# Linear attention and a two-layer MLP on one core: bf16 weights by GpSimd's DMA queue, filler matmuls and a new scheduler model

## The chip, the core and the metric

The kernel runs on one core of a Trainium2 chip. Every time in this document is device time in microseconds (us), from the start of the program to its end on that core; durations of single instructions are sometimes in nanoseconds (ns). Times of a kernel are medians of several executions. A profile is one further execution, recorded by the hardware profiler.

## The reference

Two parts are computed one after the other. The first is a linear attention with a state that decays (4 batches, 8 heads, 768 positions, 48 elements for each head); the second is an MLP over all 3072 tokens, with 384 inputs, 2048 hidden elements and 384 outputs. The inputs and outputs are float32.

```python
# attention, for every batch and head
for t in range(S):                                   # S = 768
    cur   = u * k[t] (outer) v[t]
    y[t]  = r[t] @ (state + cur)
    state = w[:, None] * state + k[t] (outer) v[t]
x = y.transpose(0, 2, 1, 3).reshape(3072, 384)

# MLP
h = x @ w_in                                         # 384 -> 2048
g = where(h >= 1, h, where(h <= -1, 0, (h + 1)**2 / 4))
out = g @ w_out                                      # 2048 -> 384
```

## The kernel before

The sequence is cut into chunks of 128 positions. A chunk of one batch is a *unit*; there are 24. In a unit, K is multiplied by inverse powers of w and R by powers of w; the products are transposed (`KR` to `RK`), the 128 x 128 scores are computed, masked (`AT`) and multiplied by V, the contribution of the state is added (`Tbd`), and a term on the diagonal with u (`VD`). The result `x` is transposed to `xT`. Two units make a block of 256 tokens; there are 12 blocks, and each block takes 8 groups of layer 1 (6 matmuls each) and 8 groups of layer 2 (4 matmuls each). The MLP uses the middle branch, (h + 1)^2 / 4, for everything; bounds on the norms are computed beside it, and the whole MLP is done again with clipping if they don't exclude an |h| above 1.

The first eight units ("soft") transpose on TensorE; the other sixteen transpose by DMA.

The order of all instructions is fixed when the kernel is built. Each operation is entered with the engines that may run it, its estimated time on each, its dependences, its buffers and a time at which it is due. A list scheduler (`Plan.run`) simulates the engines and picks engine, buffer and position. On the chip, each engine then runs its instructions in that order and waits on semaphores.

```python
# the scheduler's picture of a DMA
if o.dma is not None:
    issue = est + occ
    if len(dmas) >= 2:
        issue = max(issue, dmas[-2])
    begin = max(dma_end, issue + 0.3)
    dma_end = begin + o.dma
    ...
    o.end = dma_end + 1.7
```

```python
# constants: four loads of single 4-byte words on ScalarE's queue
def tiny(dst, src):
    for s in range(2):
        nc.scalar.dma_start(out=dst[halves[s], :], in_=src.rearrange("(p s) d -> s d p", s=2)[s])
...
tiny(wraw, w); tiny(uraw, u)

# loads of a unit (L326), SyncE's queue
nc.sync.dma_start(out=t, in_=src[b, :, t0 : t0 + C, :].rearrange("h s d -> s h d"))

# weights: float32 into a buffer (L349, L363), then a cast by DVE, ACT or POOL (L242)
ORDER = ["U0", "U1", "I0", "I1", "U2", "I2", "I3", "U3", "U4", "O0", "U5", "O1", "U6", "O2", "U7", "O3"]
t = get(bf, [128, nKb, FQ], F32)
nc.sync.dma_start(out=t, in_=w_in_src[:, :, q * FQ : (q + 1) * FQ])
...
copy(e, w_in_sb[:, kk, q * FQ : (q + 1) * FQ], bf.t[:, kk, :])
```

```python
# attention (cut): the engines that may run each step
o_kw = P.op(f"kw{i}", both, ...)                     # L390, DVE or POOL
o_rw = P.op(f"rw{i}", both, ...)                     # L394, DVE or POOL
o_v  = P.op(f"v{i}", {DVE, ACT, POOL}, ...)          # L242 V<-Vf
nc.tensor.transpose(trb.t[:, p, :], pair(krb.t, p), ident)            # L409, soft units
mm(at_p[s].t[:, p, :], rkb.t[halves[s], NP + p, :], rkb.t[halves[s], p, :], ...)   # L429, scores
nc.vector.tensor_mul(atb.t[s], at_p[s].t, umask4)                     # L435, mask
mm(pair(y, p), rkb.t[:, p, :], Tbd[b][:, p, :], ...)                  # L485, state
mm(y[:, h, :], atb.t[h % 2][:, h // 2, :], vb.t[:, h, :], ...)        # L488
mm(stb.t[:, p, :], pair(krb.t[:, H:, :], p), pair(vb.t, p), ...)      # L536, new state
o_bd = P.op(f"bd{i}", {ACT, POOL, DVE}, ...)         # L242 Tbd<-T

# MLP (cut)
mm(hb.t[:, f, :], w_in_sb[...], xT[m][:, kk, :], ...)                 # L574, layer 1
nc.scalar.activation(gb[m].t[...], hb.t, AF.Square, bias=0.5, scale=0.5)   # L586
mm(ob.t, gb[m].t[...], w_out_sb[:, f, :], ...)                        # L597, layer 2
copy(e, osb.t, ob.t)                                                  # L242 os<-o
nc.sync.dma_start(out=out[t0 : t0 + C, :], in_=osb.t)                 # L611
```

Of the kernel before, what the change touches and what calls it, by code (L numbers as in the profile page):

```python
# [8 lines left out]
F32 = mybir.dt.float32  # L9
# [5 lines left out]
SEM = 0.06  # L15


class Buf:
    def __init__(self, pool):
        self.pool, self.users, self.slot, self.t = pool, [], None, None  # L20


class Op:
    def __init__(self, name, engs, fn, deps, uses, allocs, due, dma, after, nb):
        self.name, self.engs, self.fn, self.due, self.dma = name, engs, fn, due, dma
        self.after, self.nb = [a for a in after if a], nb
        self.deps, self.uses, self.allocs = [d for d in deps if d], list(uses), list(allocs)
        self.eng = self.start = self.end = None
        for b in self.uses + self.allocs:
            b.users.append(self)  # L30


class Plan:
# [6 lines left out]
    def op(self, name, engs, fn, deps=(), uses=(), allocs=(), due=0.0, dma=None, after=(), nb=0.0):  # L40
        o = Op(name, engs, fn, deps, uses, allocs, due, dma, after, nb)
        self.ops.append(o)
        return o
# [22 lines left out]
    def run(self):  # L66
        free = dict.fromkeys(("PE", "ACT", "DVE", "POOL", "SP", "ACTQ"), 0.0)
        dmas, dma_end = [], 0.0
        todo, done, last_mlp = list(self.ops), [], "L2"
        while todo:  # L70
            cand = []
            for o in todo:
                if any(d.start is None for d in o.deps) or any(a.start is None for a in o.after):
                    continue
                pl = self.place(o) if o.allocs else (0.0, [])
                if pl is None:
                    continue
                ready = max([d.end + SEM for d in o.deps] + [a.start + 0.001 for a in o.after] + [pl[0], o.nb])
                for e in o.engs:
                    cand.append((max(free[e], ready), ready, o, e, pl[1]))  # L80
            if not cand:
                raise RuntimeError("no operation can be placed: " + ", ".join(o.name for o in todo[:12]))
# [23 lines left out]
            if o.dma is not None:  # L106
                issue = est + occ
                if len(dmas) >= 2:
                    issue = max(issue, dmas[-2])
                begin = max(dma_end, issue + 0.3)  # L110
                dma_end = begin + o.dma
                dmas.append(dma_end)
                free[e] = issue
                o.end = dma_end + 1.7
            else:
                free[e] = est + occ
                o.end = est + lat
# [8 lines left out]
def pe(t):  # L126
    return {"PE": (t, t + 0.17)}
# [22 lines left out]
def kernel(  # L150
# [11 lines left out]
    nc = tc.nc  # L162
# [16 lines left out]
    NS = 8  # L179
# [12 lines left out]
    P = Plan(slots)  # L192

# [11 lines left out]
    def row_bcast(src):  # L205
        return bass.AP(tensor=src.tensor, offset=src.offset, ap=[[0, 128], [1, H * D]])
# [3 lines left out]
    wraw = const.tile([128, NP], F32, name="wraw")  # L210
    uraw = const.tile([128, NP], F32, name="uraw")
# [36 lines left out]
    def tiny(dst, src):  # L248
        with nc.allow_non_contiguous_dma(reason="384 words"):
            for s in range(2):  # L250
                nc.scalar.dma_start(out=dst[halves[s], :], in_=src.rearrange("(p s) d -> s d p", s=2)[s])

    c_wbc = P.op("c_wbc", {"ACT": (0.6, 2.5)}, lambda e: nc.scalar.dma_start(out=w_bc, in_=row_bcast(w)), due=-100)
    c_cols = P.op("c_col", {"POOL": (0.2, 0.2)}, lambda e: nc.gpsimd.iota(i_int, pattern=[[0, 1]], base=0, channel_multiplier=1), due=-100)

    def f_kr(i):
        def fn(e):
            nc.vector.memset(KR[i], 0.0)
        return fn

    kr0 = [P.op(f"c_kr{i}", {"DVE": (0.35, 0.4)}, f_kr(i), due=-90 + i if i < 2 else 0) for i in range(slots["KR"])]

# [3 lines left out]
    c_icol = P.op("c_icol", {"DVE": (0.3, 0.35)}, f_col, deps=[c_cols], due=-99)  # L266
# [10 lines left out]
    def f_wu(e):  # L277
        nc.vector.memset(wraw, 1.0)
        nc.vector.memset(uraw, 1.0)
        nc.vector.memset(ones, 1.0)  # L280
    c_wu0 = P.op("c_wu0", {"DVE": (0.3, 0.3)}, f_wu, due=-95)

    def f_wu1(e):
        tiny(wraw, w)
        tiny(uraw, u)
    c_wu = P.op("c_wu", {"ACT": (1.8, 4.0)}, f_wu1, deps=[c_wu0], due=-99)
    c_ubc = P.op("c_ubc", {"ACT": (0.6, 4.5)}, lambda e: nc.scalar.dma_start(out=u_bc, in_=row_bcast(u)), due=-94)
# [5 lines left out]
    def f_wc(e):  # L293
        nc.scalar.activation(wc, wraw, AF.Ln)
        nc.scalar.activation(wc, wc, AF.Exp, scale=float(C))
    c_wc = P.op("c_wc", {"ACT": (0.45, 0.5)}, f_wc, deps=[c_wu], due=11)

    def f_uw(e):
        nc.gpsimd.memset(uw, 0.0)
        for s in range(2):  # L300
            nc.gpsimd.tensor_mul(uw[halves[s], :, s], wraw[halves[s]], uraw[halves[s]])
    c_uw = P.op("c_uw", {"POOL": (0.5, 0.5)}, f_uw, deps=[c_wu], due=10)

# [4 lines left out]
    c_tz = P.op("c_tz", {"POOL": (2.0, 2.0)}, f_tz, due=16)  # L308


    D_m = [13.0, 18.0, 24.0, 30.0, 36.0] + [44.0 + 12.4 * i for i in range(NB)]
# [4 lines left out]
    def add_load(i):  # L316
        b, c = units[i]
        t0 = c * C
        res = {}
        due = LD[i]  # L320
        for j, (nm, src) in enumerate((("K", k), ("R", r), ("Vf", v))):
            bf = Buf(nm)

            def fn(e, bf=bf, src=src):
                t = get(bf, [128, H, D], F32)
                nc.sync.dma_start(out=t, in_=src[b, :, t0 : t0 + C, :].rearrange("h s d -> s h d"))  # L326

            o = P.op(f"ld{nm}{i}", {"SP": (0.5, 0)}, fn, after=[loads[i - 1][nm][1] if i else None], allocs=[bf], due=due + 0.1 * j, dma=0.9)
            res[nm] = (bf, o)
        loads[i] = res  # L330

    LD = {}
    ORDER = ["U0", "U1", "I0", "I1", "U2", "I2", "I3", "U3", "U4", "O0", "U5", "O1", "U6", "O2", "U7", "O3"]
    ORDER += [f"U{i}" for i in range(8, NU)]
    pos = {s: i for i, s in enumerate(ORDER)}
    for i in range(NU):
        LD[i] = -200.0 + pos[f"U{i}"] if i < 8 else D_m[i // UB] - 16 + 2 * (i % UB)
# [4 lines left out]
    w_in_ready = {}  # L342
    w_out_ready = {}
    for q in range(NQ):
        bf = Buf("wf")

        def fn(e, bf=bf, q=q):
            t = get(bf, [128, nKb, FQ], F32)
            nc.sync.dma_start(out=t, in_=w_in_src[:, :, q * FQ : (q + 1) * FQ])  # L349

        o = P.op(f"ldI{q}", {"SP": (0.2, 0)}, fn, allocs=[bf], due=-200.0 + pos[f"I{q}"], dma=2.05)
        lst = []
        for kk in range(nKb):
            def fc(e, bf=bf, q=q, kk=kk):
                copy(e, w_in_sb[:, kk, q * FQ : (q + 1) * FQ], bf.t[:, kk, :])
            lst.append(P.op(f"cI{q}{kk}", {**dve(FQ, True), **act(FQ, False), **pool(FQ, False)}, fc, deps=[o], uses=[bf], due=D_m[0] + 1.3 * q))
        w_in_ready[q] = lst
    for q in range(NQ):
        bf = Buf("wf")

        def fn(e, bf=bf, q=q):
            t = get(bf, [128, TQ, d_out], F32)
            nc.sync.dma_start(out=t, in_=w_out_src[:, q * TQ : (q + 1) * TQ, :])  # L363

        o = P.op(f"ldO{q}", {"SP": (0.2, 0)}, fn, allocs=[bf], due=-200.0 + pos[f"O{q}"], dma=2.05)
        lst = []
        for i in range(TQ):
            def fc(e, bf=bf, q=q, i=i):
                copy(e, w_out_sb[:, q * TQ + i, :], bf.t[:, i, :])
            lst.append(P.op(f"cO{q}{i}", {**dve(d_out, True), **act(d_out, False), **pool(d_out, False)}, fc, deps=[o], uses=[bf], due=34.0 + 1.0 * q))  # L370
        w_out_ready[q] = lst
# [6 lines left out]
    def attention(i):  # L378
# [16 lines left out]
        o_rw = P.op(f"rw{i}", both, f_rw, deps=[Ro, c_wpow, o_kw], uses=[Rb, krb], due=D0 - 5.8)  # L395
# [4 lines left out]
        o_v = P.op(f"v{i}", {**dve(384, True), **act(384, False), **pool(384, False)}, f_v, deps=[Vo], uses=[Vb], allocs=[vb], due=D0 - 4)  # L400
# [14 lines left out]
        else:  # L415
# [3 lines left out]
            o_rk = P.op(f"trd{i}", {"SP": (1.7, 0)}, f_trd, deps=[o_kw, o_rw], uses=[krb], allocs=[rkb], due=D0 - 9, dma=1.4)  # L419
# [96 lines left out]
        else:  # L516
            def f_xtd(e):
                nc.sync.dma_start_transpose(out=xT[m][:, :, j * C : (j + 1) * C], in_=xb.t.rearrange("p h d -> p (h d)"))
            o_xt = P.op(f"xtd{i}", {"SP": (0.65, 0)}, f_xtd, deps=[o_x], uses=[xb], due=D0 - 5, dma=0.55)
# [9 lines left out]
        if c < NCH - 1:  # L529
# [23 lines left out]
            o_bd = P.op(f"bd{i}", {**scaled(act(192, False), 2), **scaled(pool(192, False), 2), **scaled(dve(192, True), 2)}, f_bd, deps=[o_t, o_y], due=DS - 5)  # L553
# [35 lines left out]
    def layer2(i):  # L589
# [21 lines left out]
        P.op(f"out{i}", {"SP": (0.4, 0)}, lambda e: nc.sync.dma_start(out=out[t0 : t0 + C, :], in_=osb.t), deps=[oe], uses=[osb], due=lambda ready, last: ready + 2, dma=0.5)  # L611
# [121 lines left out]
```

## Time and profile before

| | |
|---|---|
| time, median of 3 runs | 194.84 us (194.29 to 196.55) |
| span of the profiled run | 194.4 us |
| busy: TensorE (PE), its weight loads (PEld) | 164.1 us, 121.0 us |
| busy: VectorE (DVE), ScalarE (ACT), GpSimd (POOL) | 110.5, 107.9, 106.8 us |
| moved by DMA | 31.68 MB, mean 163 GB/s |

A busy time is a sum over the whole span. The profile's rows by slice give the same in 40 equal parts, one digit each (9 is 90% or more); the row PEclk has the TensorE clock that was granted, in tenths, the row DMA the mean busy share of the core's 16 DMA engines. A line of the costliest groups has the source line, the engine, the operation, the result `<-` the operands, shapes and count; then busy time and mean duration in ns; then how long the engine was idle before them and what ended the idle time. L12 is line 12 of the kernel. "SPq" and "ACTq" are the queues on which SyncE and ScalarE issue DMAs. In the chain of waits, each row has a start, a duration, and the piece of work that the end waited for.

### The profile page before, as it was taken

Reading aid. Unit: us, or ns where it says so; the run is one execution under the profiler, and the core shown is the slowest. Engines: PE = TensorE matmul, PEld = TensorE weight load, DVE = VectorE, ACT = ScalarE, POOL = GpSimd, SP = SyncE. Lnnn points to the kernel's source line nnn. Section 1 sums busy time; section 2 is a strip of 40 time slices with the busy share of each in tenths; the row PEclk is TensorE's granted clock in tenths of the full one; section 3 lists DMA queues with packets and bytes.
Section 4 is the critical chain, followed back from the end, with each engine's and each line's share of the span. In section 5 each row is a group of like instructions: output and inputs, shape, how many; then the busy total and the mean of one; then the engine's idle time right before and its main releaser. Section 6 shows DMA issues by size and latency. Waiting matters only on the chain.

```text
span 194.4 us, 4322 instructions
## 1 busy us (share of the span) xinstructions
PE 164.1 (84%) x1642; PEld 121.0 (62%) x1642; DVE 110.5 (57%) x223; ACT 107.9 (55%) x226; POOL 106.8 (55%) x155
## 2 busy tenths in 40 slices
PE   0453984988999997998997989799979999999990
PEld 0242873757777766775774767576757777777650
DVE  4669698799999957675556676586845300000000
ACT  2316573785856582866556665645665455555210
POOL 7336163567799895988769797977963000000000
PEclk9999998599999999999999999999999999999998
DMA  5999999989899968898797988888776211111121
GB/s 93 183 302 233 350 180 249 269 204 235 206 233 150 215 130 186 171 199 166 147 208 154 201 179 153 203 183 181 155 159 193 66 42 40 43 41 40 44 82 51
DMA packets 106747, 31.68 MB, mean 163 GB/s; under 512 B 99808, under 2 KB 105184, under 8 KB 106720
## 3 DMA queue, kind: packets, MB, share of 16 engines
q1 hardware_dynamic: 105600, 30.94, 70.5%
q10 hardware_dynamic: 1120, 0.40, 1.4%
q8 instruction: 15, 0.25, 0.6%
q14 instruction: 12, 0.10, 0.2%
HBM read 20.84 MB, written 4.72 MB: 131 GB/s over the span
## 4 chain that ended last, share of the span: by engine, by line
PE 45%; DMA 20%; DVE 12%; POOL 8%; SPq 6%; ACT 4%; issue 3%; DVEq 0%; POOLq 0%; ACTq 0%
PE h L574 19%; PE o L597 19%; DMA Vf<-in_v_dram 7%; DMA R<-in_r_dram 6%; DVE AT L435 4%; DMA K<-in_k_dram 4%; SPq L326 4%; DMA out_dram<-os 3%; PE a L409 2%; POOL VD L475 2%; POOL KR L394 2%; POOL KU L465 2%; DVE x L500 2%; POOL KU L464 1%; PE a L488 1%
## 5 line engine op out<-in xcount | busy, mean ns | idle before, releaser
L574 PE MATMUL h<-xT,w_in_sb 128*128 128x256 bf16 x576 | 79.6, 277 | 2.4 <-ACT g L586 1.9
L597 PE MATMUL o<-w_out_sb,g 128*128 128x384 bf16 x384 | 75.7, 326 | 1.3 <-DVE os L242 1.3
L586 ACT ACTIVATE g<-h 128x512 bf16<-128x512 f32 x96 | 56.0, 593 | 32.0 <-PE h L574 30.7
L574 PEld LDWEIGHTS <-w_in_sb 128*128 128x128 bf16 x576 | 55.2, 99 | 16.6 <-issue 3.1
L597 PEld LDWEIGHTS <-g 128*128 128x128 bf16 x384 | 35.7, 98 | 17.7 <-issue 1.4
L435 DVE TENSOR_TENSOR AT<-a,umask 128x512 bf16<-128x512 f32 x48 | 30.8, 682 | 6.5 <-PE a L429 6.3
L526 ACT ACTIVATE x<-x 128x384 bf16<-128x384 bf16 x24 | 12.5, 522 | 16.8 <-DVE x L500 16.7
L394 POOL TENSOR_TENSOR KR<-R,Wpow 128x384 bf16<-128x384 f32 x16 | 16.6, 1039 | 6.7 <-DMA R<-in_r_dram 5.5
L500 DVE TENSOR_TENSOR x<-a,VD 128x384 bf16<-128x384 f32 x24 | 13.3, 552 | 8.9 <-PE a L488 8.4
L465 POOL TENSOR_TENSOR KU<-KU,R 128x384 f32<-128x384 f32 x16 | 17.1, 1071 | 1.3
L464 POOL TENSOR_TENSOR KU<-K,u_bc 128x384 f32<-128x384 f32 x16 | 17.2, 1076 | 0.0
L475 POOL TENSOR_TENSOR VD<-V,dg 128x384 f32<-128x384 bf16 x16 | 13.6, 855 | 6.6 <-DVE dg L470 3.2
L390 DVE TENSOR_TENSOR KR<-K,Winv 128x384 bf16<-128x384 f32 x16 | 11.3, 709 | 9.1 <-DMA K<-in_k_dram 6.0
L409 PE MATMUL a<-ident,KR 128*128 128x128 bf16 x64 | 6.9, 264 | 8.0 <-DVE KR L390 6.5
L242 ACT COPY os<-o 128x384 f32<-128x384 f32 x16 | 7.6, 478 | 9.3 <-PE o L597 7.1
L242 ACT CAST V<-Vf 128x384 bf16<-128x384 f32 x15 | 7.6, 508 | 8.4 <-DMA Vf<-in_v_dram 8.3
L543 DVE TENSOR_TENSOR T<-T,a 48x192 f32<-48x192 f32 x32 | 11.1, 347 | 1.0 <-PE a L536 0.6
L429 PE MATMUL a<-RK 48*128 48x128 bf16 x192 | 10.4, 229 | 1.5 <-DVE RK L242 1.1
L536 PE MATMUL a<-V,KR 128*128 128x96 bf16 x80 | 7.3, 219 | 5.0 <-ACT V L242 2.6
L409 PEld LDWEIGHTS <-KR 128*128 128x128 bf16 x64 | 5.3, 118 | 8.9 <-DVE KR L390 6.5
L488 PE MATMUL a<-V,AT 128*128 128x48 bf16 x192 | 9.2, 189 | 1.5 <-DVE VD L457 1.3
L536 PEld LDWEIGHTS <-KR 128*128 128x128 bf16 x80 | 5.6, 105 | 6.6 <-issue 6.2
(70 smaller groups left out, 165.9 us busy)
## 6 DMA issues: line engine op xcount, KB each, us to landing
K<-in_k_dram SPq DMA_DIRECT2D x24, 192.0 KB, 4.3
R<-in_r_dram SPq DMA_DIRECT2D x24, 192.0 KB, 3.8
Vf<-in_v_dram SPq DMA_DIRECT2D x24, 192.0 KB, 4.3
out_dram<-os SPq DMA_DIRECT2D x24, 192.0 KB, 2.3
wf<-in_moe_w_in_dram SPq DMA_DIRECT2D x4, 768.0 KB, 7.0
wf<-in_moe_w_out_dram SPq DMA_DIRECT2D x4, 768.0 KB, 6.0
RK<-KR SPq DMA_TRANSPOSE x16, 3.3
xT<-x SPq DMA_TRANSPOSE x16, 2.4
```

What stands on the lines that cost most here:

```text
L242: (nc.scalar.copy if eng == "ACT" else V_ENG[eng].tensor_copy)(o, i)
L394: V_ENG[e].tensor_mul(krb.t[:, :H, 0:D], Rb.t, Wpow)
L409: nc.tensor.transpose(trb.t[:, p, :], pair(krb.t, p), ident)
L435: nc.vector.tensor_mul(atb.t[s], at_p[s].t, umask4)
L464: nc.gpsimd.tensor_mul(kub.t, Kb.t, u3)
L465: nc.gpsimd.tensor_mul(kub.t, kub.t, Rb.t)
L475: nc.gpsimd.tensor_mul(vdb.t, vb.t, dgb.t[:, :, None].to_broadcast([128, H, D]))
L500: nc.vector.tensor_add(xb.t, yb.t[:, 0:384].rearrange("p (h d) -> p h d", h=H), vdb.t)
L536: mm(stb.t[:, p, :], pair(krb.t[:, H:, :], p), pair(vb.t, p), start=True, stop=True)
L574: mm(hb.t[:, f, :], w_in_sb[:, kk, (2 * n + f) * 128 : (2 * n + f + 1) * 128], xT[m][:, kk, :], start=(kk == 0), stop=(kk == nKb - 1),)
L586: nc.scalar.activation(gb[m].t[:, 2 * n : 2 * n + 2, :], hb.t, AF.Square, bias=0.5, scale=0.5)
L597: mm(ob.t, gb[m].t[:, f, j * C : (j + 1) * C], w_out_sb[:, f, :], start=(f == 0), stop=(f == nN - 1))
```

## The change

It has four parts.

1. **A scheduler model that knows more of the DMA.** It limits a ring to 160 entries and SyncE's and ScalarE's queues to eight outstanding transfers, lets the queues share the transfer time, makes a landing later after 45 us, and adds 0.6 us to the readiness of attention matmuls from then on. Blocks are due at other times, loads are due 2 us earlier, and in the later sixteen units three steps lose their choice of engine: the R product is VectorE's, the casts of V and of the state are ScalarE's.
2. **Filler matmuls.** Products of a zero tile with itself, into a PSUM bank that nobody reads, are put wherever the model leaves TensorE free before 24 us, so that its clock is up when work arrives.
3. **No 4-byte loads.** w and u are loaded as rows; eight small transposes on TensorE turn them into the columns that `wc` and `uw` need. The broadcast of u is loaded later, on SyncE's queue.
4. **Weights cast in flight.** GpSimd issues the eight loads of the weights with a bf16 destination, so that the 28 casts and their float32 buffers go. The units' loads come first: `U0 U1 U2 U3 I0 I1 I2 I3 O0 O1 U4 O2 O3 U5 U6 U7`.

```diff
+CFG = {
+    "order": "U0 U1 U2 U3 I0 I1 I2 I3 O0 O1 U4 O2 O3 U5 U6 U7",
+    "soft": 8, "sw": True,
+    "due": [13.0, 22.0, 30.0, 36.0, 42.0], "step": 12.6,
+    "warm": 24.0, "steady": 45.0,
+}
...
+                if o.dma and "POOL" not in o.engs and len(lanes) >= 8:
+                    ready = max(ready, lanes[-8])
+                if "PE" in o.engs and ready > steady and o.name[0] != "L":
+                    ready += 0.6
+                if o.late is not None and max(free["PE"], ready) > o.late:
+                    gone.append(o)          # a filler that would come after 24 us is dropped
+                    continue
...
-                issue = est + occ
-                if len(dmas) >= 2:
-                    issue = max(issue, dmas[-2])
-                begin = max(dma_end, issue + 0.3)
-                dma_end = begin + o.dma
-                dmas.append(dma_end)
+                took, nd, wait = o.dma
+                issue, ring = est + occ, rings[e]
+                while sum(n for t, n in ring if t > issue) + nd > 160:
+                    issue = min(t for t, n in ring if t > issue)
+                begin = max(served, issue + wait)
+                served = begin + took
+                ring.append((served, nd))
                 free[e] = issue
-                o.end = dma_end + 1.7
+                o.end = served + 0.6 + (1.0 if est > steady else 0.0)
...
-        tiny(wraw, w)
-        tiny(uraw, u)
+        for i in range(2):
+            for p in range(NP):
+                nc.tensor.transpose(colb.t[:, i, p : p + 1], rows[:, i, 2 * p : 2 * p + 2, :].rearrange("q h d -> q (h d)"), onef)
...
+    for i in range(160):
+            for _ in range(2):
+                mm(wmb.t, zero, zero, start=True, stop=True, skip_group_check=True)
...
-        LD[i] = -200.0 + pos[f"U{i}"] if i < 8 else D_m[i // UB] - 16 + 2 * (i % UB)
+        LD[i] = -200.0 + pos[f"U{i}"] if f"U{i}" in pos else D_m[i // UB] - 18 + 2 * (i % UB)
...
-            nc.sync.dma_start(out=t, in_=w_in_src[:, :, q * FQ : (q + 1) * FQ])      # and 28 casts
+        if CFG["sw"]:
+                nc.gpsimd.dma_start(out=dst, in_=src)                                   # dst is bf16
+            o = P.op(f"ld{tag}{q}", {"POOL": (1.1, 0)}, fn, after=gate + prev_w[-1:], due=due, dma=(2.05, 0, 1.0))
...
-        o_rw = P.op(f"rw{i}", both, f_rw, ...)
+        o_rw = P.op(f"rw{i}", both if soft else {"DVE": both["DVE"]}, f_rw, ...)
-        o_v = P.op(f"v{i}", {**dve(384, True), **act(384, False), **pool(384, False)}, f_v, ...)
+        o_v = P.op(f"v{i}", {**act(384, False), **({**dve(384, True), **pool(384, False)} if soft else {})}, f_v, ...)
-            o_bd = P.op(f"bd{i}", {**scaled(act(192, False), 2), **scaled(pool(192, False), 2), **scaled(dve(192, True), 2)}, f_bd, ...)
+            o_bd = P.op(f"bd{i}", {**scaled(act(192, False), 2), **(scaled(pool(192, False), 2) if soft else {})}, f_bd, ...)
```

## The prediction

> **What bounds the kernel now.** I read the page's busy rows by slice first, because shares over the whole span mix three stages.
>
> ```profile
> PE   0453984988999997998997989799979999999990
> ...
> PEclk9999998599999999999999999999999999999998
> DMA  5999999989899968898797988888776211111121
> ...
> L574 PE MATMUL h<-xT,w_in_sb 128*128 128x256 bf16 x576 | 79.6, 277 | 2.4 <-ACT g L586 1.9
> L597 PE MATMUL o<-w_out_sb,g 128*128 128x384 bf16 x384 | 75.7, 326 | 1.3 <-DVE os L242 1.3
> ```
>
> Each digit covers 4.86 us. TensorE is nearly full from about 50 us to the end; before that it isn't, while the DMA row stands at 8 or 9 from the second slice. So there is a fill limited by loads, a middle in which attention and MLP share TensorE, and an end of MLP alone. I then asked for the busy time of those stretches, cut at the first MLP matmul (19.36), at 50 and 150, and at the last matmul (189.56). Columns: stretch, length, then busy time (count) of PE, PEld, DVE, ACT, POOL, then granted clock, DMA share and GB/s.
>
> ```profile
> 0.00:19.36 19.36, 6.62 (x71) 4.52 (x72) 13.02 (x30) 7.18 (x15) 9.81 (x28) 1.00 0.88 202
> 19.36:50.00 30.64, 25.77 (x300) 20.46 (x300) 25.54 (x51) 19.81 (x42) 15.98 (x25) 0.89 0.99 251
> 50.00:150.00 100.00, 92.25 (x993) 67.97 (x989) 69.96 (x138) 61.89 (x136) 81.05 (x103) 1.00 0.87 179
> 150.00:189.56 39.56, 39.47 (x294) 28.00 (x289) 1.98 (x6) 18.55 (x35) 0.00 (x0) 1.00 0.14 49
> 189.56:194.40 4.84, 0.00 (x0) 0.00 (x0) 0.00 (x0) 0.47 (x1) 0.00 (x0) 0.82 0.16 51
> ```
>
> TensorE idles 12.74 us, 4.87 us, 7.75 us, 0.09 us and 4.84 us in them. No other engine is as full in any stage, so the bound is TensorE's static order: work, plus holes, plus matmuls run slowly. The chain of waits prints an MLP group of layer 1 (6 matmuls) and one of layer 2 (4) at 0.65 to 0.66 us each in the last stage; I take 0.653. There are 96 of each: 192 x 0.653 = 125.4 us, which no part of the change touches.
>
> The same work is slower early on. Timeline, start and duration of pieces of one line:
>
> ```profile
> 10.54 1.13 PE L409 MATMUL a<-ident,KR 128*128 128x128 bf16 x8 [0.48 <-DVE T L545]
> ...
> 28.42 0.61 PE L409 MATMUL a<-ident,KR 128*128 128x128 bf16 x8
> ...
> 37.58 1.06 PE L409 MATMUL a<-ident,KR 128*128 128x128 bf16 x8
> ```
>
> Eight transposes take 1.13 us, then 0.61, then 1.06 again after a thin stretch at 30 to 35 us, where the granted clock falls to 0.72 and then 0.60. Three layer-1 groups (at 19.36, 34.93 and 36.34) pay some 0.63 us extra each, two transpose sets 0.45 each, smaller pieces perhaps 0.5: about 3.3 us after the first MLP matmul.
>
> Last, the holes of the middle stage. TensorE's waits from 50 to 150 (waiter, releaser: total, times, longest), then a piece of the chain of waits:
>
> ```profile
> PE h L574 <- ACT g L586: 1.9, 2, 1.2
> PE a L536 <- DVE V L242: 1.6, 2, 1.3
> PE a L536 <- ACT V L242: 1.2, 2, 0.9
> ```
>
> ```profile
> 135.87 5.43 DMA Vf<-in_v_dram
> 141.32 0.51 ACT V L242
> 141.84 0.50 ACT g L586
> 142.38 0.81 PE h L574 x6
> ```
>
> A V load issued at 135.87 lands 5.43 us later; ScalarE, which runs in order, is held at the cast of V, the squaring behind it is held too, and TensorE waits 1.19 us for it. The holes are late loads handed on by in-order queues, not too little capacity.
>
> [...] The two `wraw` and two `uraw` loads are such; they took 5.1 and 4.6 us to land for 0.8 KB each, and SyncE's issue of the first V beside them took 2.76 us against 0.58 for the next. [...]
>
> **The change part by part.**
>
> *Four-byte loads.* They go, and 8 small transposes with a few tiny operations replace them off the early path. `lw` started at 4.72 after waiting 2.70 us for w, and the first R landed at 6.84. I estimate 1 to 1.5 us earlier for the first operands.
>
> *Filler matmuls.* The built order holds 232, of which 96 come first and 210 before the first MLP matmul. At the warm spacing (0.61 minus 0.17 us of pipeline, over 8 = 0.055 us) 210 take 11.6 us[...]. The attention matmuls ordered before the first MLP matmul occupy about 4.3 us by the warm rows (4 sets of transposes at 0.44, 4 state products at 0.17, 3 score sets at 0.23, and the rest). With a start at 1.1 us: 1.1 + 11.6 + 1.7 + 4.3 = 18.7 us if nothing waits. Waits will be there, so I take the first MLP matmul at 21 us, 1.6 later than before. In exchange the clock is up: of the 3.3 us of slow matmuls I keep 0.3. The other 22 fillers cost 1.2 us if their holes are not real.
>
> *Weights by GpSimd with the cast in flight.* Twenty-eight casts go: ScalarE 3.9 + 3.5, GpSimd 3.2 + 3.1, VectorE 1.5 + 0.8, together 16.0 us, nearly all before 52 us. None lies on TensorE directly, but they stand ahead of masks and copies in the queues (the chain has 0.83 us at 22.75 and 1.08 at 41.35). [...] if each takes the 1.1 us that the diff writes down for it (no trace here has measured one), that is 8.8 us against the 6.3 it loses. They come after five operations of units 0 to 2, so at about 11 us. Their 6.3 MB at the 253 GB/s that the page's slices from 9.7 to 48.6 us average take 25 us: the last lands at 36 us or, with half the engines' time given to the unit loads, later. The last float32 weight was issued at 44.95 before and landed near 50. So weights come no later than before for the second layer, and TensorE's new order, which runs both first blocks' layer 1 before most of layer 2, fits that.
>
> *Earlier attention.* Two more sets of transposes, two state products and one score set precede the first MLP matmul: 2 x 0.44 + 2 x 0.17 + 0.23 = 1.45 us moved forward. From the stage table, attention after 19.36 is 92.25 - 112 groups x 0.653 = 19.1 us in the middle plus 25.77 - 20 x 0.653 - 3.3 = 9.4 us before 50, so 28.5; it becomes 27.0.
>
> *Scheduler model.* It books waits for outstanding loads, adds slack to attention matmuls after 45 us, moves loads two microseconds ahead, and gives the casts of V and of the state to ScalarE alone and the R product to VectorE alone. ScalarE has the room: 61.89 of 100 us in the middle, less the casts removed. I expect the middle's 7.75 us of holes to become 4, and the 4.87 of 19 to 50 us to become 3.
>
> *Sum.* Before, as a test of the terms: 19.36 + 125.4 + 28.5 + 3.3 + 4.87 + 7.75 + 4.84 = 194.0, against a span of 194.4. After: 21 + 125.4 + 27.0 + 1.2 + 0.3 + 3 + 4 + 4.8 = **186.7 us**.
>
> **The rivals.**
>
> *GpSimd's queue is slow.* [...] the weights arrive some 8 us late and TensorE, in order, waits at layer 1 or 2 with attention stuck behind. For it: GpSimd is busy 52% of the fill even before, and VectorE is the fullest engine of 19 to 50 us (25.54 of 30.64) after TensorE. Against it: the two streams of weights have some 10 us of slack. It would make 191 to 195.
>
> *The fill is bound by bandwidth anyway.* DMA share is 0.99 there and the bytes read are the same; then loads only trade places, and attention of units 4 to 7 starves in place of the weights. Against it: TensorE has 32 groups, 21 us of MLP, from the first four units alone. This gives 188 to 191.
>
> *ScalarE becomes the new hold.* With every late V on one in-order engine that also frees the h banks, holes of the 142 us kind may grow. Then the middle keeps 7 to 9 us of holes and the total is 190 to 192.
>
> *Everything fits*, the middle as dense as the end: 181 to 183.
>
> **Range and chances.** The middle case is 186.7. The gain rests on closing about 5.6 us of holes and 3 us of slow clock, paid for by 2.8 us of later start and fillers. Half-success on the holes gives 189.5, so the range is 181.5 to 192. Two per cent below 194.84 is 190.9; only the first rival, or two together, reach it. I put faster at 0.78, within 2% at 0.16, slower at 0.06.
>
> **What would show each step.** Right: eight transposes near 0.61 us from the first on; first MLP matmul at 20 to 22 us; no granted clock below 1 between 30 and 40 us; weight casts gone; TensorE busy above 95 of 100 us from 50 to 150; V no longer ahead of an MLP wait. Wrong: TensorE waiting on the weight tiles; eight GpSimd issues taking much more than 9 us; the fillers still running when K and R have landed; ScalarE's squaring ahead of larger TensorE waits. The total would miss most if one of the two weight streams arrives after its place in the order.

## The result, and the profile after

The changed kernel takes **187.76 us** (median of 3 runs, 187.32 to 188.23) against 194.84 us. The ratio is 0.962, with a 95% interval of 0.952 to 0.972; measured again beside its variants it was 0.963 (0.956 to 0.971). The span of the profiled run fell from 194.4 to 186.4 us. The two profiled executions took 196.34 and 188.23 us, 8.1 us apart where the medians are 7.1 us apart; so about 1 us of the 8.0 us by which the spans differ is not the change's.

The same views as before, first the page's rows by slice and its two MLP lines (4.66 us to a digit now):

```profile
PE   7999975899999999999999999899799999999970
...
PEclk9999999699999999999999999999999999999996
DMA  5999999999985999998999977979999951111111
...
L614 PE MATMUL h<-xT,w_in_sb 128*128 128x256 bf16 x576 | 78.5, 275 | 1.0 <-ACT g L626 1.0
L637 PE MATMUL o<-w_out_sb,g 128*128 128x384 bf16 x384 | 76.8, 326 | 0.3 <-ACT g L626 0.2
```

The leading 7999 is mostly fillers. TensorE then has one dent, in the sixth and seventh slices, and is full from there on. By stretches, cut at the first MLP matmul (21.25), at 50 and 150, and at the last matmul (180.67); busy us (count) of PE, PEld, DVE, ACT, POOL, then clock, DMA share, GB/s:

```profile
0.00:21.25 21.25, 19.80 (x321) 18.65 (x322) 15.63 (x37) 10.25 (x20) 13.86 (x30) 1.00 0.94 164
21.25:50.00 28.75, 24.85 (x266) 19.20 (x264) 14.76 (x34) 14.66 (x29) 5.27 (x9) 0.94 1.15 186
50.00:150.00 100.00, 98.01 (x1052) 72.13 (x1049) 72.64 (x142) 71.14 (x158) 75.45 (x89) 1.00 1.03 177
150.00:180.67 30.67, 30.67 (x254) 22.41 (x251) 4.79 (x11) 15.34 (x29) 0.00 (x0) 1.00 0.18 57
180.67:186.40 5.73, 0.01 (x1) 0.00 (x0) 0.00 (x0) 0.48 (x1) 0.00 (x0) 0.71 0.13 43
```

The middle's holes went from 7.75 to 1.99 us. Asked by tile, the matmuls of the MLP show where the 8.0 us of span came from. At 50 us, 16 groups of layer 1 and 10 of layer 2 are done, against 16 and 3 before: 7 groups, 4.6 us. But attention is some 50 matmuls behind by then: TensorE's busy time after 50 us, less the MLP groups still to come, is 20.3 us against 18.7. So the fill gains 3.0 us and the holes after 50 us 5.9, and the tail gives back 0.9. What is left in the middle, as waits of TensorE from 50 to 150 us:

```profile
PE h L614 <- ACT g L626: 1.0, 1, 1.0
PE a L576 <- ACT V L275: 0.6, 1, 0.6
```

The dent in the fill is new. Chain of waits (start, us, what):

```profile
15.85 16.93 DMA Vf<-in_v_dram
...
33.22 0.50 PE a L576 x4
33.73 1.28 PE h L614 x6
```

V of unit 4 needs 16.93 us to land, and TensorE, in order, waits 2.53 us for it. The first MLP group behind it then takes 1.28 us and not 0.65. The stretches say why: the granted clock is 0.50 there.

```profile
30.00:33.30 3.30, 0.77 (x16) 0.47 (x15) 0.49 (x2) 1.01 (x3) 0.00 (x0) 0.94 1.27 185
33.30:36.00 2.70, 2.70 (x25) 2.11 (x26) 2.43 (x6) 0.60 (x1) 0.38 (x1) 0.50 1.27 184
```

Why V is late stands in two rows of GpSimd's timeline and three of SyncE's:

```profile
14.40 3.24 POOL L396 DMA_DIRECT2D w_in_sb<-in_moe_w_in_dram  x4
17.64 3.00 POOL L396 DMA_DIRECT2D w_out_sb<-in_moe_w_out_dram  x4
```

```profile
17.91 4.79 SPq L366 DMA_DIRECT2D K<-in_k_dram  x1
22.74 4.14 SPq L366 DMA_DIRECT2D R<-in_r_dram  x1
26.92 7.35 SPq L366 DMA_DIRECT2D Vf<-in_v_dram  x1
```

SyncE issues the fifteen loads of units 0 to 4 in 17.1 us (0.74 to 17.86), and needs 16.4 us for the next three (17.91 to 34.27), while GpSimd's eight weight loads are in flight. Taken as rates of issue, that is 15 x 192 KB in 17.1 us, 172 GB/s, and then 3 x 192 KB in 16.4 us, 36 GB/s. The profile counts 3,712 packets and 3.15 MB on GpSimd's queue, 849 bytes to a packet, and on the queue q1, which has the loads of the units, 102,032 packets and 24.85 MB, 244 bytes to a packet. That the second queue gets ahead of the first shows in the landings of w_out and V below (32.00 and 32.78 us); by what rule the two share the DMA engines no run shows.

### The profile page after: what moved, and what is told of

Read it like the earlier page. It is cut to its first block, busy times and chain, and to the rows that moved or that the text cites. A ratio compares the mean times of both kernels' runs of the same rounds, so it can differ in the third digit from the quotient of the medians.

```text
span 186.4 us, 4812 instructions
## 1 busy us (share of the span) xinstructions
PE 173.3 (93%) x1882; PEld 132.4 (71%) x1882; DVE 107.8 (58%) x221; ACT 111.9 (60%) x237; POOL 94.6 (51%) x128
## 3 DMA queue, kind: packets, MB, share of 16 engines
q1 hardware_dynamic: 102032, 24.85, 75.0%
q0 software_dynamic: 3712, 3.15, 10.5%
## 4 chain that ended last, share of the span: by engine, by line
PE 57%; DMA 18%; SPq 13%; POOL 3%; issue 3%; ACT 2%; DVE 1%; POOLq 0%; DVEq 0%; ACTq 0%
PE o L637 25%; PE h L614 24%; DMA Vf<-in_v_dram 13%; SPq L366 11%; DMA R<-in_r_dram 2%; PE a L469 2%; DMA K<-in_k_dram 2%; PE a L528 1%; PE a L525 1%; POOL VD L515 1%; PE a L576 1%; ACT g L626 1%; PE a L449 1%; SPq L558 1%; POOL KU L505 1%
## 5 line engine op out<-in xcount | busy, mean ns | idle before, releaser
L637 PEld LDWEIGHTS <-g 128*128 128x128 bf16 x384 | 35.4, 98 | 16.4 <-ACT g L626 1.5
L504 POOL TENSOR_TENSOR KU<-K,u_bc 128x384 f32<-128x384 f32 x16 | 18.6, 1163 | 2.3 <-DMA K<-in_k_dram 2.3
L338 PE MATMUL o<-zero 128*128 128x128 bf16 x232 | 18.0, 237 | 1.0 <-DVE zero L308 1.0
L434 DVE TENSOR_TENSOR KR<-R,Wpow 128x384 bf16<-128x384 f32 x20 | 15.4, 771 | 5.0 <-DMA R<-in_r_dram 4.8
L338 PEld LDWEIGHTS <-zero 128*128 128x128 bf16 x232 | 15.4, 108 | 1.4 <-DVE zero L308 1.0
L588 POOL TENSOR_TENSOR T<-T,wc 128x192 f32<-128x192 f32 x16 | 8.2, 525 | 12.4 <-DVE T L583 12.2
L430 DVE TENSOR_TENSOR KR<-K,Winv 128x384 bf16<-128x384 f32 x15 | 9.5, 631 | 8.3 <-DMA K<-in_k_dram 7.4
L430 POOL TENSOR_TENSOR KR<-K,Winv 128x384 bf16<-128x384 f32 x9 | 9.0, 999 | 10.0 <-DMA K<-in_k_dram 10.0
L275 ACT CAST V<-Vf 128x384 bf16<-128x384 f32 x19 | 9.6, 507 | 6.5 <-DMA Vf<-in_v_dram 6.4
L275 ACT CAST Tbd<-T 48x192 bf16<-48x192 f32 x34 | 11.8, 346 | 2.7 <-PE a L525 1.5
L275 ACT COPY RK<-a 128x1024 bf16<-128x1024 bf16 x7 | 7.1, 1009 | 7.1 <-PE a L449 6.9
```

Of the source, the lines that this page charges most:

```text
L275: (nc.scalar.copy if eng == "ACT" else V_ENG[eng].tensor_copy)(o, i)
L338: mm(wmb.t, zero, zero, start=True, stop=True, skip_group_check=True)
L430: V_ENG[e].tensor_mul(krb.t[:, H:, 0:D], Kb.t, Winv)
L434: V_ENG[e].tensor_mul(krb.t[:, :H, 0:D], Rb.t, Wpow)
L504: nc.gpsimd.tensor_mul(kub.t, Kb.t, u3)
L637: mm(ob.t, gb[m].t[:, f, j * C : (j + 1) * C], w_out_sb[:, f, :], start=(f == 0), stop=(f == nN - 1))
```

## The experiments

Each set of runs had its own runs of the kernel before (medians 196.07, 198.14 and 196.49 us), so times are compared as ratios to those. Ratios and their intervals leave out executions more than 1.5% above the fastest of the same kernel, and medians do not; E7's ratio rests for that reason on two of its four runs (184.66 and 185.25 us, without 187.66 and 189.81). E1, E3 and E7 shared a set with the changed kernel:

> The changed kernel once more, as the base for its variants on the same chip: 187 to 188.5 us, ratio to before 0.955 to 0.97.

It came to 0.963 (0.956 to 0.971), 189.15 us.

### E1: without the fillers

```diff
         def f_wm(e, i=i):
-            if wmb.t is None:
-                get(wmb, [128, 128], F32)
-            for _ in range(2):
-                mm(wmb.t, zero, zero, start=True, stop=True, skip_group_check=True)
+            pass
```

> The changed kernel with its 232 filler matmuls not issued; every other instruction stays in its place in the order. Theory: the fillers pay, because the attention of the first units and the first MLP groups run at the full clock; without them eight transposes take about 1.1 us again and the first MLP groups near 1.4 us, and the time rises by 1 to 2.5 us. Rival: the first MLP matmul waits for the first quarter of w_in anyway (it landed at 20.9 us), the slow attention hides under that wait, and the 22 fillers after it are saved; then the first MLP matmul stays at 21 to 21.5 us and the time is within 0.7 us of the changed kernel.

Measured: 189.54 us, ratio 0.968 (0.963 to 0.973), which overlaps the base. TensorE's timeline:

```profile
7.79 1.03 PE L446 MATMUL a<-ident,KR 128*128 128x128 bf16 x8
...
19.40 1.08 PE L446 MATMUL a<-ident,KR 128*128 128x128 bf16 x8
20.27 1.49 PE L611 MATMUL h<-xT,w_in_sb 128*128 128x256 bf16 x6
```

With fillers the first transposes are fast but late:

```profile
9.33 0.61 PE L449 MATMUL a<-ident,KR 128*128 128x128 bf16 x8
```

So the fillers do lift the clock, products of zeros included: 0.61 us for eight transposes at 9.33, 1.03 to 1.08 without them until 19.4. (The column for the granted clock has 1.00 for the first 21.25 us of both runs, so only the durations show the slow clock there.) But the first 96 take 7.70 us (0.99 to 8.69), while the operands of unit 0 are ready at 7.21. Without them the first MLP matmul comes 1 us *earlier*, and three groups are slow (1.49, 1.44, 1.11 us). The two nearly cancel. The rival named the right size, though not its reason: the first MLP matmul did move.

### E3: the weights by SyncE, in float32, with casts

```diff
-    "sw": True,
+    "sw": False,
```

> The changed kernel with its weights loaded in float32 by SyncE and cast by VectorE, ScalarE and GpSimd, as before; order of loads, scheduler model and fillers stay. Theory: the 28 casts (16 us over three engines) stand ahead of attention in the in-order queues and cost 2 to 5 us. Rival: they fill idle time of engines off the path; and with GpSimd's queue gone the loads of units 4 and 5 are no longer starved (V of unit 4 took 16.93 us to land), so the time is within 1 us or even lower.

Measured: 185.44 us, ratio **0.948** (0.943 to 0.952), below the changed kernel's interval. The theory falls: the cast in flight is no gain here. The stretch from 21.25 to 50 us:

```profile
21.25:50.00 28.75, 26.66 (x300) 19.64 (x295) 22.07 (x47) 18.70 (x40) 15.31 (x24) 1.00 1.04 265
```

The casts are back (GpSimd is busy 15.31 and not 5.27 us, VectorE 22.07 and not 14.76), yet TensorE has 2.1 us of holes in this stretch and not 3.9, and the clock stays up. This is not because V of unit 4 comes sooner. It is issued at 27.17 us, needs 6.5 us and lands at 33.70, later than in the changed kernel (32.78). But TensorE's order, which the scheduler built anew, has nine MLP groups from 28.12 us on ahead of unit 4, and no wait in front of it:

```profile
34.13 0.82 PE L614 MATMUL h<-xT,w_in_sb 128*128 128x256 bf16 x6
34.79 0.61 PE L449 MATMUL a<-ident,KR 128*128 128x128 bf16 x8
35.24 0.33 PE L576 MATMUL a<-V,KR 128*128 128x96 bf16 x4
```

What differs is how far the plan is off. When the kernels are built, `Plan.run` books the landing of this V at 31.55 us in E3, 2.2 us too early; in the changed kernel it books 25.40 us, 7.4 us too early, and TensorE's order relies on it.

### E7: GpSimd's weights kept, two units ahead of w_out

```diff
-    "order": "U0 U1 U2 U3 I0 I1 I2 I3 O0 O1 U4 O2 O3 U5 U6 U7",
+    "order": "U0 U1 U2 U3 I0 I1 I2 I3 U4 U5 O0 O1 O2 O3 U6 U7",
```

> The changed kernel with the w_out quarters issued by GpSimd after the loads of units 4 and 5 in the order, not before. Theory (GpSimd's weights starve the unit loads): V of unit 4 lands well before 32.8 us, the hole of 2.53 us and the slow clock behind it go, and the time falls by 1.5 to 3 us. Rival (the fill is bound by bytes, whoever goes first): the w_out quarters land later, TensorE waits for them in layer 2 instead, and the time is within 1 us or higher.

Measured: 186.45 us, ratio **0.945** (0.939 to 0.951). Chain of waits and stretch:

```profile
15.52 13.31 DMA Vf<-in_v_dram
```

```profile
21.25:50.00 28.75, 27.35 (x336) 22.25 (x334) 21.10 (x47) 16.89 (x34) 11.48 (x18) 1.00 1.15 189
```

The same V lands 4 us sooner (28.83, booked at 25.40), the holes are 1.4 us, the clock stays at 1.00. E3 and E7 agree within their intervals, with casts and without, so no gain or loss from the cast in flight itself can be seen. What they share is a plan that is nearer to the chip at this place. The changed kernel's plan books both queues as one line, in which V of unit 4 is served before all of w_out; the chip serves the second queue beside the first, and the first quarter of w_out, issued 1.8 us after V, landed before it (32.00 us). That this error cost the changed kernel its 1.6 to 1.9% is likely, but not isolated: both variants have TensorE's order built anew, and no run corrects the booking alone. E3 and E7 are the fastest versions found here, 5.2 and 5.5% below the kernel before, and cannot be told apart.

### E5, E6 and B2: which part of the scheduler model closed the middle

E5 gives the later units their choice of engine back:

```diff
-  o_rw: both if soft else {"DVE": both["DVE"]}
+  o_rw: both
-  o_v:  {**act(384, False), **({**dve(384, True), **pool(384, False)} if soft else {})}
+  o_v:  {**dve(384, True), **act(384, False), **pool(384, False)}
-  o_bd: {**scaled(act(192, False), 2), **(scaled(pool(192, False), 2) if soft else {})}
+  o_bd: {**scaled(act(192, False), 2), **scaled(pool(192, False), 2), **scaled(dve(192, True), 2)}
```

> The changed kernel with the engine choices of before given back in the later sixteen units (R product on VectorE or GpSimd; casts of V and of the state on any of the three). Theory: the middle is dense because the model adds slack and loads come earlier, not because of these choices; the holes of TensorE from 50 to 150 us stay at 1 to 4 us and the time within 1.5 us of the changed kernel. Rival: putting every cast of V and of the state on ScalarE is what closed the holes; then they grow back to 5 to 8 us and the time rises by 3 to 5 us.

E6 drops the slack and the late landing:

```diff
-                    ready += 0.6
+                    ready += 0.0
...
-                o.end = served + 0.6 + (1.0 if est > steady else 0.0)
+                o.end = served + 0.6 + 0.0
```

> The changed kernel without the 0.6 us of slack for attention matmuls and without the 1.0 us of later landing after 45 us. Theory: these two are what closed the holes of the middle; they grow back from 2.0 us to 5 us or more and the time rises by 3 to 5 us. Rival: the loads being due 2 us earlier, or the limits on outstanding transfers, are enough; then holes stay below 4 us and the time within 1.5 us.

B2 adds two lines to the kernel before:

```diff
+                if "PE" in o.engs and ready > 45.0 and o.name[0] != "L":
+                    ready += 0.6
...
-  D_m[i // UB] - 16 + 2 * (i % UB)
+  D_m[i // UB] - 18 + 2 * (i % UB)
```

> The kernel before with two lines of the scheduler change alone: 0.6 us of slack for attention matmuls after 45 us, and loads due 2 us earlier. Theory: TensorE's holes from 50 to 150 us fall from 7.75 to 2 to 4 us and the time by 3 to 5 us. Rival: the old picture of the DMA still places loads too late, and nothing moves by more than 1.5 us.

Measured: E5 0.974 (0.963 to 0.985), E6 0.971 (0.959 to 0.983), B2 1.005 (1.002 to 1.009). In the middle TensorE is busy 96.93 us in E5 and 95.68 in E6. The row of B2:

```profile
50.00:150.00 100.00, 91.77 (x959) 66.79 (x954) 77.44 (x145) 59.82 (x131) 80.09 (x95) 0.98 0.88 178
```

So the holes are 3.1, 4.3 and 8.2 us. E5 and E6 lie above the changed kernel, but their intervals overlap its own. E6's holes grew less than its theory said and more than its rival allowed; E5's stayed within its theory, though its ratio lies 1.1% above the changed kernel's, some 2 us where 1.5 at most were expected. In E6 the new waits of the middle are for DMA transposes, 2.6 us in five pieces, of the kind that slack is there for:

```profile
PE a L469 <- DMA RK<-KR: 2.6, 5, 1.2
```

B2 settles that slack and earlier loads are not enough on their own: holes as before, and half a per cent slower.

### B4 and B5: the picture of the DMA alone, and all of the scheduler change

B4 is the kernel before with the booking of DMAs replaced (the time that an issue takes on SyncE included), and with the output stores due at other times:

```diff
-                issue = max(issue, dmas[-2]) ...; begin = max(dma_end, issue + 0.3); o.end = dma_end + 1.7
+                (ring of 160, eight outstanding, shared `served`, as in the change)
-  loads dma=0.9;             out dma=0.5,           due ready + 2
+  loads dma=(1.05, 64, 0.6); out dma=(0.8, 8, 0.6), due oe.end - 12
```

> The kernel before with the scheduler's new picture of the DMA alone (ring and queue limits, shared transfer time, longer transfers, landing, position of the output stores); no slack, loads due as before, engine choices as before. Theory, after slack and earlier loads alone gave nothing: the old picture put loads where the chip could not serve them, so this part alone takes TensorE's holes from 50 to 150 us from 7.75 to 3 to 5 us and the time down by 2 to 4 us (ratio 0.98 to 0.99). Rival: no part works alone; holes stay at 6 us or more and the ratio within 0.01 of 1.

B5 adds the slack, the earlier loads and the fixed engines to B4.

> The kernel before with all of the scheduler change in the middle: picture of the DMA, slack of 0.6 us, loads due 2 us earlier, fixed engines in the later units. Weights, their casts, the load order, the due times of the blocks, the 4-byte loads stay; no fillers. Theory: holes from 50 to 150 us of 1.5 to 3 us, as in the changed kernel, and a ratio of 0.965 to 0.975; what is left to the changed kernel with weights by SyncE (0.948) is the fill. Rival: the due times and the load order of the changed kernel are needed too; holes above 4 us and a ratio above 0.98.

Measured: B4 191.48 us, **0.980** (0.975 to 0.985); B5 191.61 us, 0.988 (0.974 to 1.001). The middle of B4:

```profile
50.00:150.00 100.00, 97.94 (x1025) 72.15 (x1024) 74.41 (x141) 66.07 (x143) 80.84 (x101) 1.00 1.00 183
```

The picture of the DMA, with the place of the output stores, takes the holes from 7.75 to 2.06 us and the time down by 2%. The waits that the prediction read in the middle shrink with it. There, TensorE waited 3.6 us for V and 1.9 for `g` behind it; in B4 this is left of them:

```profile
PE a L541 <- DVE V L247: 0.8, 1, 0.8
```

Which of the terms does it (limits, longer transfers, landing, output stores) no run separates; the limits (160 entries, eight transfers) are the program's own figures, and no run shows them of the chip. With slack, early loads and fixed engines on top, 0.59 us of holes are left, and no time is measurably saved: B5's span is 189.7 us, B4's 189.6, and B5's expected ratio of 0.965 to 0.975 was missed. Both keep a fill like the kernel before, with a mean clock of 0.88 from 21 to 50 us. So the rest of the changed kernel's gain is to be looked for in the fill.

### E4: the 4-byte loads put back

```diff
+    tiny(wraw, w); tiny(uraw, u)       # after the rows of w and u, on ScalarE's queue; nobody reads them
```

> The changed kernel with the four 4-byte loads issued again on ScalarE's queue behind the rows of w and u; nobody reads them. The first traces had w at 4.72 us with them and 4.76 us without, and an issue of the first V of 2.76 and 2.69 us. If the 4-byte loads cost the fill nothing, w lands within 0.2 us of 4.76, the first R product starts within 0.3 us of 6.65 and the first MLP matmul within 0.5 us of 21.25. If they cost what I had predicted, the R product starts 1 to 1.5 us later.

A single profiled run. ScalarE's timeline:

```profile
2.87 4.25 ACTq L287 DMA_DIRECT2D uraw<-in_u_dram  x2
...
7.17 0.52 ACT L349 ACTIVATE lw<-w_bc 128x384 f32<-128x384 f32 x1 [5.14 <-DMA R<-in_r_dram]
```

The row of w is there at 4.70 (VectorE reads it then), but ScalarE is still issuing 4-byte loads until 7.12; `lw` starts at 7.17 in place of 4.76, and the R product at 8.87 in place of 6.65. The first MLP matmul moves by only 0.8 us, to 22.04. So the same loads cost the first R product 2.2 us here, and at most 0.28 us in the kernel before (6.93 against 6.65, where it waited for R to land). In both they stand between the load of w and `lw` in ScalarE's order; the two for u held it for 4.25 us here and for 1.41 us there, and why stays open. The run as a whole took 185.76 us. In it V of unit 4 came 1.4 us sooner and TensorE's hole was 1.43 us:

```profile
31.79 0.34 PE L584 MATMUL a<-V,KR 128*128 128x96 bf16 x4 [1.43 <-DVE V L275]
```

The six matmuls behind it took 0.82 us with their pipeline, against 1.48 at the same place in the changed kernel, and the mean clock from 21.25 to 50 us was 1.00, against 0.94. One run is too little to call it faster; but with a hole 1.1 us shorter than the changed kernel's 2.53 the fill kept its clock. The first V's issue took 2.62 us here, 2.69 in the changed kernel and 2.76 before, so the 4-byte loads were not what held it.

### E8 and E9: two tries at a better fill

E8 puts w_in earlier on GpSimd and starts with 64 fillers; E9 has float32 weights on SyncE in another order, with the same 64 fillers.

```diff
E8: "order": "U0 U1 U2 I0 I1 U3 I2 I3 U4 U5 O0 O1 O2 O3 U6 U7"
E9: "order": "U0 U1 U2 U3 I0 I1 I2 I3 O0 U4 O1 U5 O2 O3 U6 U7", "sw": False
both: pe(0.11) -> pe(0.22 if i < 16 else 0.11)
```

> The changed kernel with GpSimd issuing the first w_in quarters before its products of unit 2, the w_out quarters after units 4 and 5, and the first 16 filler steps booked at twice their time (64 fillers at the start in place of 96). If the first MLP matmul waits for w_in and the fillers, it comes at 18 to 19.5 us in place of 21.3, and the time is 1.5 to 3 us below that of the kernel with the units first (ratio 0.93 to 0.94). If bytes bound the fill, units 3 to 5 come later instead and the time equals that kernel's (0.945).

> The changed kernel with float32 weights on SyncE's queue in one planned order with the units (U4 before the second quarter of w_out, U5 before the third), casts by the engines, and 64 fillers at the start in place of 96. If one planned queue is what the fill needs and the fillers held it back, the ratio is 0.935 to 0.945, below both the changed kernel (0.963) and its variants with weights by SyncE (0.948) or units first (0.945). If the fill is bound by bytes whatever the order, it equals these two.

E8 came to 0.956 (0.945 to 0.968). Its first MLP matmul is 3.3 us earlier, just under the 18 to 19.5 us expected, and the time is not better than E7's:

```profile
17.93 0.82 PE L614 MATMUL h<-xT,w_in_sb 128*128 128x256 bf16 x6
...
24.98 0.40 PE L449 MATMUL a<-ident,KR 128*128 128x128 bf16 x4 [2.27 <-POOL KR L430]
```

With the weights earlier, K of a later unit is late: GpSimd waits 7.49 us for it and forms its product at 23.93 us. TensorE waits 2.27 us for that, and the matmuls from 25.93 us on are slow: four state products take 0.53 us at 26.55, against 0.33 at 35.02, and the mean clock from 21.25 to 50 us is 0.94. E9 came to 0.972 (0.959 to 0.985), not the 0.935 to 0.945 expected: from 21 to 50 us TensorE waits for casts of w_out, which it did not in E3:

```profile
PE o L637 <- POOL w_out_sb L275: 2.0, 4, 0.9
```

E8 shows a start bought with later units, E9 an order that is worse than E3's, although both change the fillers as well. Neither shows a fill that is free of waits.

## Why the prediction was right, and where it was not

The kernel took 187.76 us against 186.7 predicted, inside the range. The terms of the sum, with what they measured in the profile of 186.4 us:

| term | predicted | measured |
|---|---|---|
| first MLP matmul | 21 | 21.25 |
| MLP, 192 groups at 0.653 | 125.4 | 125.4 (0.65 to 0.66 each again) |
| attention after it | 27.0 | 25.4 |
| fillers after it | 1.2 | 1.2 |
| slow clock after it | 0.3 | 1.5 |
| holes to 50 us | 3 | 3.9 |
| holes from 50 to 150 us | 4 | 2.0 |
| tail | 4.8 | 5.7 |
| sum | 186.7 | 186.4 |

The attention term is what remains of TensorE's busy time after MLP, fillers and slow clock; the slow clock is the excess of the pieces between 33.2 and 37.2 us over their warm durations.

- **TensorE's order as the bound: right.** From 50 us to the last matmul it is busy 128.7 of 130.7 us. That the terms add up shows nothing more after the change, as attention is the remainder.
- **Filler matmuls: the cost right, the worth too high.** The start at 21 us was worked out from their count. I had traded it for 3 us of slow clock as if that were their doing. E1 puts their worth at 0.5% with overlapping intervals, because they delay unit 0 by about what they save. The 1.7 us that the sum for the start has beside the warm spacing was my estimate for a slow beginning of the fillers; in the trace the first 40 start within 4.2 us, 0.11 us each, and the other 56 are through 3.5 us later, 0.06 each. That the fillers were still running (until 8.69 us) when K and R had landed (the R product started at 6.65) was one of the prediction's signs of being wrong.
- **Weights by GpSimd: the step that failed.** I counted the 16 us of casts as the good side and a slow GpSimd queue as the risk. The issues began at 14.40 us and not at about 11, and took 0.75 to 0.94 us each, all eight 6.24 us, less than the 8.8 estimated. TensorE did not wait for a weight tile. I had written that "TensorE's new order ... fits that". It does not: the plan has V of unit 4 at 25.40 us, beside the weights it lands at 32.78, TensorE stands in its order, and the clock falls to 0.50 where I had forecast none below 1 from 30 to 40 us. E3 and E7, whose plans are less wrong there, are each faster. My second rival had units starving in place of weights, and I had set it aside. It is half the mechanism: in E3 V comes later still, and costs nothing where the order expects it.
- **4-byte loads: too high.** I expected 1 to 1.5 us for the first operands and the R product came 0.28 us earlier. I had also read SyncE's 2.76 us for the first V as their doing; without them it is 2.69.
- **Scheduler model: the size of the effect right, the cause partly wrong.** I expected 7.75 to become 4 and named slack, earlier loads and fixed engines beside the booked waits. B4 shows that the booking of the DMAs, with the place of the output stores, works without the rest. B2 shows slack with earlier loads to be worth nothing on their own, and B5 that the additions on top bring no measurable time.
- **ScalarE as the new hold: did not happen.** Its busy time in the middle rose from 61.89 to 71.14 us, and the largest wait behind it is 1.0 us.

The failures cancel: less from fillers, weights and 4-byte loads, more from the middle. That the total came within 1.1 us is therefore luck in part. The chances were also laid out too narrowly: I wrote that only the first rival or two together reach 190.9 us, but my own figures for the second (up to 191) and for ScalarE (up to 192) reach it too.

Open: what share of the fill's gain is due to the order of loads and what to the due times of the blocks, since no run changed the due times alone; which term of the DMA picture closes the holes; and whether, in E5 and E6, slack and fixed engines are worth a per cent in the changed kernel, where the intervals overlap.

## What to carry to other kernels

In a statically ordered kernel, correct the scheduler's picture of the slowest shared thing first: here, the new booking of transfers, with the place of the output stores, was worth 2% alone, slack and earlier loads without it nothing. A transfer moved to another queue can leave the planned order: here the first quarter of w_out, issued 1.8 us after V of unit 4, landed 0.8 us before it. So compare the landings that the plan books with those of the trace, and if both queues carry what an in-order engine waits for, try them on one queue (E3), or hold the bulk one back until the small loads are issued (E7). Fillers for a cold TensorE delay the work once its operands are ready: here the 96 at the start ended 1.5 us after that.

## What the runs showed of the hardware that I had not expected

- After waits of 2.27 to 2.53 us in a thin stretch the granted clock fell to half, though not always at once. In the changed kernel (TensorE busy 0.77 of 3.3 us, wait of 2.53 us) it was 0.50 from 32.9 to 36.2 us. In E1 the six matmuls behind a wait of 2.30 us still took 0.82 us; behind the next wait, 0.65 us, twelve took 2.73 us from 35.10 on, against 1.47 at 38.73. In E8 four transposes behind a wait of 2.27 us took 0.40 us, and the next four, behind 0.56 us more, 0.60. After waits of 1.43 and 0.66 us in E4, twelve matmuls took 1.47 us. In the middle the longest wait was 2.0 us in E8 and in B2 both, and the mean clock of 50 to 150 us was 1.00 in E8 and 0.98 in B2; so the length of the wait alone may not settle it.
- Products of a zero tile lifted the clock: eight transposes behind them took 0.61 us at 9.33 us, against 1.03 without them at 7.79.
- Two loads of 192 four-byte words each held ScalarE's queue for 4.25 us in E4 and for 1.41 us in the kernel before, at nearly the same place in its order.
